# Attention on one Trainium2 core: ones beside the value tiles, every shift on GpSimd, normalisation on ScalarE, loads by 8 heads

## The chip, the cores and the metric

The kernel runs on one core of a Trainium2 chip. The metric is the device time of one execution in microseconds (us); lower is better. Each core has five engines with their own instruction queues: TensorE (PE; its weight loads are listed apart as PEld), VectorE (DVE), ScalarE (ACT), GpSimd (POOL) and SyncE (SP), which here only issues DMAs. The 16 DMA engines of the core move data between HBM and the on-chip memory SBUF. Matmul results go to PSUM.

## The reference

```python
B, H, Sq, Sk, D = 16, 32, 192, 1024, 128        # q: (B,H,Sq,D); k, v: (B,H,Sk,D); bf16

def reference(q, k, v):
    scale = q.shape[-1] ** -0.5
    scores = jnp.einsum("bhqd,bhkd->bhqk", q, k) * scale
    p = _softmax(scores, axis=-1)
    return jnp.einsum("bhqk,bhkd->bhqd", p, v)
```

There are 512 independent heads, and each is a whole softmax attention of 192 queries over 1024 keys.

## The kernel before

**Units.** Two heads make a pair, and a pair makes three units of 128 rows by 1024 keys: queries 0 to 127 of the first head (j = 0), queries 0 to 127 of the second (j = 1), and the last 64 queries of both heads stacked (j = 2). There are 256 pairs and 768 units. In the code `k3` is this j before the change.

**What is done to a unit.** `qk` (TensorE) makes the scores of the unit in PSUM (`s_ps`, two buffers), as two matmuls of 512 columns, for j = 2 as two column-tiled pairs. `rowmax` (VectorE, L300) copies them to SBUF (`ss`, four buffers), times minus the scale, and keeps the row's minimum in `nb`. Then a unit goes one of two ways, by `ROUTES = (R_W, R_W, R_EA)`. Units j = 0 and 1 (`R_W`): GpSimd subtracts the minimum (`shift`, L188, a tensor_tensor against a broadcast column) into `x_sb`; TensorE transposes in eight blocks of 128x128 (`tr`, L244) into `pt_ps`; ScalarE takes the exponential on the way out of PSUM into `pt_sb` (`evac`, L367). Unit j = 2 (`R_EA`): ScalarE takes the exponential before the transposes (`exp_first`, L356), with the row sums as a by-product in `rs`, and copies behind them (L369). `pv` (TensorE) multiplies the eight transposed blocks with the value tiles `vs` into `o_ps` (L267 for j = 0, 1; L273 and L275 for j = 2). For `R_W` units each such matmul is followed by one with a single column of ones against the same weights (L270), which gathers the row sums in slot 3 of `o_ps`. `onorm` (VectorE, L327 and L330) takes the reciprocals of a pair's sums and multiplies the pair's three outputs into `ob`.

**Order.** Each engine's program is written out by hand, one step a unit, with lags: in a step TensorE does `qk` of unit step+1, `tr` of unit step-4 and `pv` of unit step-7. VectorE does `rowmax` of the step's unit and `onorm` 8 steps behind the pair's last unit. Semaphores carry the dependences: `s_qk`, `s_max`, `s_xp` and `s_xa`, `s_tr`, `s_eva`, `s_pv`, `s_on`.

**Loads and stores.** All DMAs are issued by SP, in one order. A group is G = 16 heads, and NS = 2 groups have buffers, 32 heads in all. `loads(g)` issues the transposing load of K (L141, 4 MB), that of Q (L144, 0.79 MB) and the plain load of V (L149, 4 MB); for each partition and head, V's 8 rows of 128 values are 2,048 bytes in one run in HBM and in `vs` alike. Ahead of K it waits until the scores of the group that held the buffer are done, ahead of V until that group's `pv` is. `stores(g)` waits for the group's normalised output and issues three DMAs (L158, L163, L164), 0.79 MB in runs of 256 bytes. The order is `loads(g + NS)`, then `stores(g)`, for each g.

Of the kernel before, what the change touches and what calls it, by code (L numbers as in the profile page):

```python
# [6 lines left out]
F32 = mybir.dt.float32  # L7
ACT_FN = mybir.ActivationFunctionType
ALU = mybir.AluOpType

R_EA = 0
R_ED = 1
R_W = 2


def _attention_kernel(nc, q, k, v, out, G=16, NS=2, LAGS=(2, 4, 5, 7), ROUTES=(R_W, R_W, R_EA)):
# [4 lines left out]
    assert NH % G == 0 and G % 2 == 0  # L21
# [3 lines left out]
    NU = NGR * UPG  # L25
    KT_TILES = SK // 128
    scale = float(D) ** -0.5

    L_X, L_TR, L_EV, L_PV = LAGS
    assert 1 <= L_X < L_TR < L_EV < L_PV  # L30
# [4 lines left out]
    NRS = 4  # L35

# [5 lines left out]
    def route(u):  # L42
        return ROUTES[u % len(ROUTES)]

    x_cnt = []
    ev_cnt = []
    n_xa = n_xp = n_ea = n_ed = 0
    for u in range(NU):
        r = route(u)
        if r == R_W:  # L50
            n_xp += 1
            x_cnt.append(n_xp)
        else:
            n_xa += 1
            x_cnt.append(n_xa)
        if r == R_ED:
            n_ed += 1
            ev_cnt.append(n_ed)
        else:
            n_ea += 1  # L60
            ev_cnt.append(n_ea)

    with ExitStack() as es:
# [11 lines left out]
        vs = sb("vs", [128, NS, G, KT_TILES, 128], BF16)  # L75
        ob = sb("ob", [128, NSO, PPG, 4, 128], BF16)
# [3 lines left out]
        pt_sb = sb("pt_sb", [128, NPT, KT_TILES, 128], BF16)  # L80
# [5 lines left out]
        pt_ps = [ps("pt_ps%d" % i, [128, KT_TILES, 128], BF16) for i in range(2)]  # L86
        o_ps = [ps("o_ps%d" % i, [128, 4, 128], F32) for i in range(2)]
# [7 lines left out]
        s_xa = sem("s_xa")  # L95
        s_xp = sem("s_xp")
        s_tr = sem("s_tr")
        s_eva = sem("s_eva")
        s_evd = sem("s_evd")
# [6 lines left out]
        def unit_info(u):  # L106
            pr = u // 3
            k3 = u % 3
            g = pr // PPG
            pg = pr % PPG  # L110
            return pr, k3, g, pg

        O_SLOT = (0, 2, 1)

        def load_cnt(g):
            return 16 * (g // NS + 1)

        def store_cnt(g):
            return 48 * (g // NSO + 1)

        def wait_x(eng, u):
            if route(u) == R_W:
                eng.wait_ge(s_xp, x_cnt[u])
            else:
                eng.wait_ge(s_xa, x_cnt[u])

        def wait_evac(eng, u):
            if route(u) == R_ED:
                eng.wait_ge(s_evd, ev_cnt[u])
            else:  # L130
                eng.wait_ge(s_eva, ev_cnt[u])

        @block.sync
        def _(e):
            def loads(g):
                s = g % NS
                last_u = (g - NS + 1) * UPG - 1
                h0 = g * G
                if g >= NS:
                    e.wait_ge(s_qk, last_u + 1)  # L140
                e.dma_start_transpose(  # L141
                    kt[:, s], kf[h0:h0 + G].rearrange("g k d -> (g k) d")
                ).then_inc(sxk[s], 16)
                e.dma_start_transpose(  # L144
                    qt[:, s], qf[h0:h0 + G].rearrange("g k d -> (g k) d")
                ).then_inc(sxq[s], 16)
                if g >= NS:
                    e.wait_ge(s_pv, last_u + 1)
                e.dma_start(  # L149
                    vs[:, s], vf[h0:h0 + G].rearrange("g (p t) d -> p g t d", t=KT_TILES)  # L150
                ).then_inc(svl[s], 16)

            def stores(g):
                so = g % NSO
                e.wait_ge(s_on, (g + 1) * PPG)
                h0 = g * G
                og = of[h0:h0 + G]
# [10 lines left out]
            for g in range(NGR):  # L168
                if g + NS < NGR:
                    loads(g + NS)  # L170
                stores(g)
            for so in range(min(NSO, NGR)):
                n_uses = len(range(so, NGR, NSO))
                e.wait_ge(sst[so], 48 * n_uses)

        @block.gpsimd
        def _(gp):
# [4 lines left out]
            ).then_inc(s_setup, 1)  # L182

            def shift(u):
                gp.wait_ge(s_max, u + 1)
                if u >= NX:
                    gp.wait_ge(s_tr, u - NX + 1)
                gp.tensor_tensor(  # L188
                    x_sb[:, u % NX, :], ss[:, u % NSS, :],
                    nb[:, u % NSS: u % NSS + 1].to_broadcast([128, SK]), ALU.subtract,  # L190
                ).then_inc(s_xp, 1)

            for u in range(NU):
                if route(u) == R_W:
                    shift(u)

        @block.tensor
        def _(pe):
            def qk(u):
                pr, k3, g, pg = unit_info(u)  # L200
                s = g % NS
                if u % UPG == 0:
                    pe.wait_ge(sxk[s], load_cnt(g))
                    pe.wait_ge(sxq[s], load_cnt(g))
# [6 lines left out]
                for c in range(2):  # L211
                    cs = slice(512 * c, 512 * c + 512)
                    if k3 < 2:
                        x = a if k3 == 0 else b
                        ins = pe.matmul(  # L215
                            S[:, cs],
                            qt[:, s, x * SQ: x * SQ + 128],
                            kt[:, s, x * SK + 512 * c: x * SK + 512 * c + 512],
                            start=True, stop=True,
                        )  # L220
                    else:
                        pe.matmul(  # L222
                            S[0:64, cs],
                            qt[:, s, a * SQ + 128: a * SQ + 192],
                            kt[:, s, a * SK + 512 * c: a * SK + 512 * c + 512],
                            start=True, stop=True, tile_position=(0, 0),
                        )
                        ins = pe.matmul(  # L228
                            S[64:128, cs],
                            qt[:, s, b * SQ + 128: b * SQ + 192],  # L230
                            kt[:, s, b * SK + 512 * c: b * SK + 512 * c + 512],
                            start=True, stop=True, tile_position=(0, 64),
                        )
                ins.then_inc(s_qk, 1)

            def tr(u):
                wait_x(pe, u)
                if u >= 2:
                    wait_evac(pe, u - 2)
                X = x_sb[:, u % NX, :]  # L240
                PT = pt_ps[u % 2]
                ins = None
                for t in range(KT_TILES):
                    ins = pe.transpose(PT[:, t, :], X[:, t: SK: KT_TILES], ident[:])  # L244
                ins.then_inc(s_tr, 1)

            def pv(u):
                pr, k3, g, pg = unit_info(u)
                s = g % NS
                if u % UPG == 0:  # L250
                    pe.wait_ge(svl[s], load_cnt(g))
                wait_evac(pe, u)
                if k3 == 0 and pr >= 2:
                    pe.wait_ge(s_on, pr - 1)
                O = o_ps[pr % 2]
                PTS = pt_sb[:, u % NPT]
                sl = O_SLOT[k3]
                a = 2 * pg
                b = 2 * pg + 1
                ins = None  # L260
                with_rs = route(u) == R_W
                for t in range(KT_TILES):
                    first = t == 0
                    last = t == KT_TILES - 1
                    if k3 < 2:
                        x = a if k3 == 0 else b
                        ins = pe.matmul(O[:, sl, :], PTS[:, t, :], vs[:, s, x, t, :],  # L267
                                        start=first, stop=last, skip_group_check=True)
                        if with_rs:
                            ins = pe.matmul(O[:, 3, sl: sl + 1], PTS[:, t, :], ones[:, 0:1],  # L270
                                            start=False, stop=last, skip_group_check=True)
                    else:
                        pe.matmul(O[0:64, sl, :], PTS[:, t, 0:64], vs[:, s, a, t, :],  # L273
                                  start=first, stop=last, skip_group_check=True, tile_position=(0, 0))
                        ins = pe.matmul(O[64:128, sl, :], PTS[:, t, 64:128], vs[:, s, b, t, :],  # L275
                                        start=first, stop=last, skip_group_check=True, tile_position=(0, 64))
                        if with_rs:
                            pe.matmul(O[0:64, 3, sl: sl + 1], PTS[:, t, 0:64], ones[:, 0:1],
                                      start=False, stop=last, skip_group_check=True, tile_position=(0, 0))
                            ins = pe.matmul(O[64:128, 3, sl: sl + 1], PTS[:, t, 64:128], ones[:, 0:1],  # L280
                                            start=False, stop=last, skip_group_check=True, tile_position=(0, 64))
                ins.then_inc(s_pv, 1)

            pe.wait_ge(s_setup, 2)
# [10 lines left out]
        def _(dve):  # L295
# [9 lines left out]
            def evac(u):  # L305
                dve.wait_ge(s_tr, u + 1)
                if u >= NPT:
                    dve.wait_ge(s_pv, u - NPT + 1)
                dve.tensor_copy(pt_sb[:, u % NPT], pt_ps[u % 2][:]).then_inc(s_evd, 1)

            ri_total = [0]

            def onorm(pr):
                g = pr // PPG
                pg = pr % PPG
                so = g % NSO
                dve.wait_ge(s_pv, 3 * pr + 3)
                if pg == 0 and g >= NSO:
                    dve.wait_ge(sst[so], store_cnt(g - NSO))
# [96 lines left out]
```

## Time and profile before

| | us |
|---|---|
| median of 3 runs | 1264.91 |
| lowest, highest | 1264.91, 1265.55 |
| span of the profiled execution, first to last instruction | 1263.1 |
| PE busy; PEld busy | 1234.2; 1009.4 |
| DVE busy; ACT busy; POOL busy | 1102.0; 1048.6; 960.4 |
| first matmul starts | 21.0 |

The profiled execution is read by its span, 1263.1 us; the median of the runs stands 1.8 us above it, and what lies outside the span has no row. Busy times are sums over one execution. Matmuls are pipelined, so TensorE's busy time is not its time at peak. A DMA's issue (SPq rows) can last long because the queue takes no more until earlier transfers have drained. One pair takes 4.80 us in the steady state, and eight pairs (16 heads) take 38.4 us.

### The profile page before, as it was taken

Reading aid. Unit: us, or ns where it says so; the run is one execution under the profiler, and the core shown is the slowest. Engines: PE = TensorE matmul, PEld = TensorE weight load, DVE = VectorE, ACT = ScalarE, POOL = GpSimd, SP = SyncE. Lnnn points to the kernel's source line nnn. Section 1 sums busy time; section 2 is a strip of 40 time slices with the busy share of each in tenths; the row PEclk is TensorE's granted clock in tenths of the full one; section 3 lists DMA queues with packets and bytes.
Section 4 is the critical chain, followed back from the end, with each engine's and each line's share of the span. In section 5 each row is a group of like instructions: output and inputs, shape, how many; then the busy total and the mean of one; then the engine's idle time right before and its main releaser. Section 6 shows DMA issues by size and latency. Waiting matters only on the chain.

```text
span 1263.1 us, 48658 instructions
## 1 busy us (share of the span) xinstructions
PE 1234.2 (98%) x20480; PEld 1009.4 (80%) x20480; DVE 1102.0 (87%) x2304; ACT 1048.6 (83%) x1281; POOL 960.4 (76%) x518
## 2 busy tenths in 40 slices
PE   3999999999999999999999999999999999999997
PEld 1888888888888888888888888888888888888886
DVE  2889888898988989898898988889898898989885
ACT  1888888888888888888888888888888888888886
POOL 2778777777877778787777877777787777878774
PEclk9999999999999999999999999999999999999999
DMA  9999999999999999999999999999999999999941
GB/s 288 268 261 240 278 280 266 288 270 245 254 269 261 279 233 255 281 275 262 261 230 272 271 276 268 252 251 272 272 267 281 253 263 252 271 261 281 244 118 27
DMA packets 790743, 321.89 MB, mean 255 GB/s; under 512 B 724992, under 2 KB 724992, under 8 KB 790528
## 3 DMA queue, kind: packets, MB, share of 16 engines
q1 hardware_dynamic: 790528, 318.78, 108.8%
q8 instruction: 164, 2.69, 0.8%
q14 instruction: 51, 0.42, 0.1%
HBM read 134.22 MB, written 25.17 MB: 126 GB/s over the span
## 4 chain that ended last, share of the span: by engine, by line
PE 97%; SPq 1%; DMA 1%; ACT 0%; issue 0%; DVE 0%; ACTq 0%
PE pt_ps L244 33%; PE o_ps L267 24%; PE s_ps L215 18%; PE o_ps L273 11%; PE s_ps L222 9%; SPq L141 1%; DMA vs<-in_v_dram 1%; PE o_ps L270 1%; PE o_ps L275 1%; SPq L144 0%; PE s_ps L228 0%; ACT x_sb L356 0%; ACT pt_sb L367 0%; DVE ob L330 0%; DVE rinv L327 0%
## 5 line engine op out<-in xcount | busy, mean ns | idle before, releaser
L188 POOL TENSOR_TENSOR x_sb<-ss,nb 128x1024 bf16<-128x1024 f32 x512 | 959.7, 1895 | 288.9 <-PE pt_ps L244 266.8
L300 DVE TENSOR_SCALAR_CACHE_REDUCE ss<-s_ps 128x1024 f32<-128x1024 f32 x768 | 938.5, 1222 | 140.5 <-PE s_ps L215 110.8
L244 PEld LDWEIGHTS pt_ps<-ident,x_sb 128*128 128x128 bf16 x6144 | 487.1, 148 | 203.3 <-issue 105.4
L367 ACT ACTIVATE pt_sb<-pt_ps 128x1024 bf16<-128x1024 bf16 x512 | 521.0, 1018 | 41.9 <-PE pt_ps L244 41.8
L244 PE MATMUL pt_ps<-ident,x_sb 128*128 128x128 bf16 x6144 | 520.7, 228 | 0.2 <-ACT pt_sb L367 0.2
L267 PE MATMUL o_ps<-vs,pt_sb 128*128 128x128 bf16 x4096 | 403.0, 217 | 0.3 <-DMA vs<-in_v_dram 0.3
L369 ACT ACTIVATE pt_sb<-pt_ps 128x1024 bf16<-128x1024 bf16 x256 | 262.1, 1024 | 140.1 <-PE pt_ps L244 140.0
L270 PE MATMUL o_ps<-ones,pt_sb 128*128 128x1 bf16 x4096 | 376.0, 165 | 0.0
L267 PEld LDWEIGHTS o_ps<-vs,pt_sb 128*128 128x128 bf16 x4096 | 352.3, 97 | 0.5 <-DMA vs<-in_v_dram 0.4
L270 PEld LDWEIGHTS o_ps<-ones,pt_sb 128*128 128x128 bf16 x4096 | 340.7, 96 | 0.0
L215 PE MATMUL s_ps<-kt,qt 128*128 128x512 bf16 x1024 | 305.3, 379 | 21.3 <-DMA qt<-in_q_dram 21.0
L356 ACT ACTIVATE x_sb<-ss,nb 128x1024 bf16<-128x1024 f32 x256 | 292.3, 1142 | 23.6 <-DVE ss L300 23.6
L273 PE MATMUL o_ps<-vs,pt_sb 128*64 128x128 bf16 x2048 | 162.3, 222 | 0.0
L275 PE MATMUL o_ps<-vs,pt_sb 128*64 128x128 bf16 x2048 | 162.3, 222 | 0.0
L222 PE MATMUL s_ps<-kt,qt 128*64 128x512 bf16 x512 | 153.2, 381 | 0.6 <-DVE ss L300 0.5
L228 PE MATMUL s_ps<-kt,qt 128*64 128x512 bf16 x512 | 153.2, 381 | 0.0
L330 DVE TENSOR_TENSOR ob<-o_ps,rinv 128x384 bf16<-128x384 f32 x256 | 142.7, 557 | 8.7
L273 PEld LDWEIGHTS o_ps<-vs,pt_sb 128*64 128x64 bf16 x2048 | 121.0, 109 | 17.1
L275 PEld LDWEIGHTS o_ps<-vs,pt_sb 128*64 128x64 bf16 x2048 | 121.0, 109 | 0.0
L215 PEld LDWEIGHTS s_ps<-kt,qt 128*128 128x128 bf16 x1024 | 63.3, 96 | 23.6 <-issue 21.5
L300 DVE DVE_READ_ACCUMULATOR ss<-s_ps 128x1 f32 x768 | 64.0, 83 | 0.0
L356 ACT ACTIVATION_READ_ACCUMULATOR x_sb<-ss,nb 128x1 f32 x256 | 48.9, 191 | 0.0
(11 smaller groups left out, 165.7 us busy)
## 6 DMA issues: line engine op xcount, KB each, us to landing
vs<-in_v_dram SPq DMA_DIRECT2D x32, 4096.0 KB, 15.2
out_dram<-ob SPq DMA_DIRECT2D x32, 512.0 KB, 15.9
out_dram<-ob SPq DMA_DIRECT2D x64, 128.0 KB, 4.9
kt<-in_k_dram SPq DMA_TRANSPOSE x32, 21.4
qt<-in_q_dram SPq DMA_TRANSPOSE x32, 6.6
```

The lines of the kernel that those rows point to most:

```text
L188: gp.tensor_tensor(x_sb[:, u % NX, :], ss[:, u % NSS, :], nb[:, u % NSS: u % NSS + 1].to_broadcast([128, SK]), ALU.subtract,).then_inc(s_x ...
L215: ins = pe.matmul(S[:, cs], qt[:, s, x * SQ: x * SQ + 128], kt[:, s, x * SK + 512 * c: x * SK + 512 * c + 512], start=True, stop=True,)
L222: pe.matmul(S[0:64, cs], qt[:, s, a * SQ + 128: a * SQ + 192], kt[:, s, a * SK + 512 * c: a * SK + 512 * c + 512], start=True, stop=True, ...
L244: ins = pe.transpose(PT[:, t, :], X[:, t: SK: KT_TILES], ident[:])
L267: ins = pe.matmul(O[:, sl, :], PTS[:, t, :], vs[:, s, x, t, :], start=first, stop=last, skip_group_check=True)
L270: ins = pe.matmul(O[:, 3, sl: sl + 1], PTS[:, t, :], ones[:, 0:1], start=False, stop=last, skip_group_check=True)
L273: pe.matmul(O[0:64, sl, :], PTS[:, t, 0:64], vs[:, s, a, t, :], start=first, stop=last, skip_group_check=True, tile_position=(0, 0))
L275: ins = pe.matmul(O[64:128, sl, :], PTS[:, t, 64:128], vs[:, s, b, t, :], start=first, stop=last, skip_group_check=True, tile_position=(0, ...
L300: dve.tensor_scalar(ss[:, u % NSS, :], s_ps[u % 2][:], -scale, None, ALU.mult, ALU.min, accum_out=nb[:, u % NSS: u % NSS + 1],).then_inc(s ...
L356: act.activation(x_sb[:, u % NX, :], ss[:, u % NSS, :], ACT_FN.Exp, bias=nb[:, u % NSS: u % NSS + 1], scale=-1.0, accum_out=rs[:, pr % NRS ...
L367: act.activation(pt_sb[:, u % NPT], pt_ps[u % 2][:], ACT_FN.Exp, scale=-1.0).then_inc(s_eva, 1)
L369: act.activation(pt_sb[:, u % NPT], pt_ps[u % 2][:], ACT_FN.Copy).then_inc(s_eva, 1)
```

## The change

- **Row sums.** `vs` gets rows of `VW = 130` values instead of 128, and GpSimd writes ones into the two spare columns once at the start. A `pv` matmul takes 129 columns, so that column 128 of its output is the row sum. The matmuls of L270 are gone.
- **One way for all units.** `TYPES = (W, W, W)`: GpSimd shifts all 768 units, ScalarE takes all exponentials behind the transposes. The shift is a tensor_scalar, times -1 plus `nb`, instead of a tensor_tensor; the exponential no longer has a scale of -1.
- **Normalisation.** VectorE does one reciprocal a pair; ScalarE does three multiplications a pair (Copy with a scale per row), each counted in `s_on`.
- **Loads.** G = 8 and NS = 4, again 32 heads of buffers. K and Q still go as one transposing DMA each a group; V goes as one DMA a head, whose destination has 128 values and a gap of 2 (runs of 256 bytes). Stores still go by 16 heads (`GO`).

The lags are as before. The core of the diff:

```diff
-def _attention_kernel(nc, q, k, v, out, G=16, NS=2, LAGS=(2, 4, 5, 7), ROUTES=(R_W, R_W, R_EA)):
+TYPES = (W, W, W)
+def _attention_kernel(nc, q, k, v, out, G=8, NS=4, GO=16, L_X=2, L_TR=4, L_EV=5, L_PV=7):
...
+    VW = D + 2
...
-        vs = sb("vs", [128, NS, G, KT_TILES, 128], BF16)
+        vs = sb("vs", [128, NS, G, T, VW], BF16)
...
-        o_ps = [ps("o_ps%d" % i, [128, 4, 128], F32) for i in range(2)]
+        o_ps = [ps("o_ps%d" % i, [128, 3, VW], F32) for i in range(2)]
...
                 if g >= NS:
                     e.wait_ge(s_pv, last_u + 1)
-                e.dma_start(
-                    vs[:, s], vf[h0:h0 + G].rearrange("g (p t) d -> p g t d", t=KT_TILES)
-                ).then_inc(svl[s], 16)
+                for i in range(G):
+                    e.dma_start(
+                        vs[:, s, i, :, 0:D], vf[h0 + i].rearrange("(p t) d -> p t d", t=T)
+                    ).then_inc(svl[s], 16)
...
             for g in range(NGR):
                 if g + NS < NGR:
                     loads(g + NS)
-                stores(g)
+                if (g + 1) % (GO // G) == 0:
+                    stores((g + 1) // (GO // G) - 1)
...
+            gp.memset(vs[:, :, :, :, D:VW], 1.0).then_inc(s_setup, 1)
...
-                gp.tensor_tensor(
+                gp.tensor_scalar(
                     x_sb[:, u % NX, :], ss[:, u % NSS, :],
-                    nb[:, u % NSS: u % NSS + 1].to_broadcast([128, SK]), ALU.subtract,
-                ).then_inc(s_xp, 1)
+                    -1.0, nb[:, u % NSS: u % NSS + 1], ALU.mult, ALU.add,
+                ).then_inc(s_x[W], 1)
...
-                        ins = pe.matmul(O[:, sl, :], PTS[:, t, :], vs[:, s, x, t, :],
-                                        start=first, stop=last, skip_group_check=True)
-                        if with_rs:
-                            ins = pe.matmul(O[:, 3, sl: sl + 1], PTS[:, t, :], ones[:, 0:1],
-                                            start=False, stop=last, skip_group_check=True)
...
+                for t in range(T):
+                    for r, m, x in rows:
+                        tp = {} if j < 2 else {"tile_position": (0, r)}
+                        ins = pe.matmul(
+                            O[r:r + m, sl, 0:D + 1], P[:, t // 2, t % 2, r:r + m], vs[:, s, x, t, 0:D + 1],
+                            start=t == 0, stop=t == T - 1, skip_group_check=True, **tp)
...
+            def recip(pr):
                 dve.wait_ge(s_pv, 3 * pr + 3)
+                if pr >= 2:
+                    dve.wait_ge(s_on, ON * (pr - 1))
...
+                        src = o_ps[pr % 2][:, c, D]
+                    dve.reciprocal(rinv[:, pr % 2, c], src).then_inc(s_ri, 1)
...
-                dve.tensor_tensor(
-                    ob[:, so, pg, 0:3, :],
-                    o_ps[pr % 2][:, 0:3, :],
-                    rinv[:, pr % 2, 0:3].unsqueeze(2).to_broadcast([128, 3, 128]),
-                    ALU.mult,
-                ).then_inc(s_on, 1)
...
+            def norm(pr):
+                so = pr // PPO % NSO
+                act.wait_ge(s_ri, RECIPS * (pr + 1))
+                if pr % PPO == 0 and pr // PPO >= NSO:
+                    act.wait_ge(sst[so], 48 * (pr // PPO // NSO))
+                for sl in range(3):
+                    act.activation(
+                        ob[:, so, pr % PPO, sl, :], o_ps[pr % 2][:, sl, 0:D], ACT_FN.Copy,
+                        scale=rinv[:, pr % 2, sl:sl + 1],
+                    ).then_inc(s_on, 1)
+            for step in range(NU + L_PV + 3):
                 u = step - L_EV
-                if 0 <= u < NU and route(u) != R_ED:
+                if 0 <= u < NU:
                     evac(u)
...
+                u = step - L_PV - 1
+                if 0 <= u < NU and u % 3 == 2:
+                    norm(u // 3)
```

## The prediction

> **What bounds the kernel now.** First the page: engine shares, the slices, the chain that ended last, and the costliest groups.
>
> ```profile
> PE 1234.2 (98%) x20480; PEld 1009.4 (80%) x20480; DVE 1102.0 (87%) x2304; ACT 1048.6 (83%) x1281; POOL 960.4 (76%) x518
> ...
> DMA  9999999999999999999999999999999999999941
> ...
> q1 hardware_dynamic: 790528, 318.78, 108.8%
> q8 instruction: 164, 2.69, 0.8%
> ...
> PE 97%; SPq 1%; DMA 1%; ACT 0%; issue 0%; DVE 0%; ACTq 0%
> ...
> L188 POOL TENSOR_TENSOR x_sb<-ss,nb 128x1024 bf16<-128x1024 f32 x512 | 959.7, 1895 | 288.9 <-PE pt_ps L244 266.8
> ```
>
> The chain is TensorE for 97%. But the DMA engines are full in every slice up to the last two, and the chain alone can't tell how near they are to bounding. So next the timeline of SP's own queue, for one 16-head group and the start of the next (start, us, instruction):
>
> ```profile
> 902.61 18.25 SPq L141 DMA_TRANSPOSE kt<-in_k_dram  x1
> 920.91 3.98 SPq L144 DMA_TRANSPOSE qt<-in_q_dram  x1
> 924.93 0.59 SPq L149 DMA_DIRECT2D vs<-in_v_dram  x1
> 925.57 4.52 SPq L158 DMA_DIRECT2D out_dram<-ob  x1
> 930.13 9.94 SPq L163 DMA_DIRECT2D out_dram<-ob  x1
> 940.12 0.64 SPq L164 DMA_DIRECT2D out_dram<-ob  x1
> 940.80 17.73 SPq L141 DMA_TRANSPOSE kt<-in_k_dram  x1
> ```
>
> SP goes from one DMA to the next with no gap. The long rows are not waits for compute (the scores that this K load needs had ended at 901.5): the last stores of the run, with nothing in front of them, issue in 0.4 to 1.3 us each, so L163's 9.9 us is V still draining. K of the fourth group issues at 101.85 and of the 26th at 940.80: 22 cycles of 38.1 us. TensorE needs 38.4 us for 16 heads. Two resources are within 1% of each other; a change that relieves one and loads the other goes by the other.
>
> Third, the windows view, for the rates (window, length, ..., DMA share, GB/s): a K load alone at the start, V alone, the last stores alone.
>
> ```profile
> 6.00:16.00 10.00, 0.00 (x0) 0.00 (x0) 0.00 (x0) 0.00 (x0) 0.00 (x0) 1.00 1.28 290
> ...
> 626.00:632.00 6.00, 6.00 (x104) 4.97 (x104) 5.16 (x12) 4.74 (x7) 3.90 (x3) 1.00 1.05 396
> ...
> 1258.50:1260.50 2.00, 0.00 (x0) 0.00 (x0) 0.00 (x0) 0.00 (x0) 0.00 (x0) 0.79 0.97 220
> ```
>
> V, in packets of 2,048 bytes, moves at 396 GB/s. K's transposes, in packets of 256, at 290: 256 B / (290/16 GB/s) = 14.1 ns a packet and engine. The stores, plain copies with rows of 256 bytes, at 220: 18.6 ns.
>
> **TensorE.** The chain in order of time gives the pitch of a value matmul:
>
> ```profile
> 603.36 0.05 PE o_ps L273
> ...
> 604.77 0.08 PE o_ps L267
> ```
>
> With a ones matmul behind it one takes 0.080 us, without (j = 2) 0.055. The change takes away 16 such followers a pair: 16 x 0.025 = 0.39 us; the 129th column adds 1/128 of 0.055 to 24 pitches, 0.01. A pair goes from 4.80 to 4.42 us, 16 heads from 38.4 to 35.4, the run loses 256 x 0.38 = 97 us. Rows that start 260 bytes apart have no row here; at worst the gain is lost (the old 0.080 pitch). K and Q for 8 heads in place of 16 let the first matmul start at about 11.4 us instead of 21.0: 9.6 more. TensorE alone would end at 1263.1 - 97 - 10 = 1156 us.
>
> **V's loads: the term that decides.** A run of V in `vs` shrinks from 2,048 to 256 bytes by the gap of two ones. The packet size of the old load equals the shorter of its two runs (2,048 in HBM, far longer in `vs`), so I take packets of 256 now, eight times as many: 16,384 for 16 heads. 16 heads of V are 4.19 MB. At 396 GB/s that is 10.6 us; at the transposes' 14.1 ns, 14.5 us; at the stores' 18.6 ns, 19.0 us. Neither row is a plain load of 256-byte rows; one shares its direction, the other its form, so I take the middle, 16.8.
>
> The Trainium skill ("DMA: Bandwidth & Descriptors", Why small descriptors are slow) counts 8 + 3 cycles for a 256-byte packet, 12.9 ns at its 850 MHz; an estimate from that page would be 13.2 us for V, a cycle of 39.7 and, by the sum below, 1290 us. Both rows here are slower than it says, and its Specifications ask for 512 bytes for full rate, which speaks against this change.
>
> **Instruction fetches.** The 164 packets of q8 are 16 KB each, and TensorE has 40,960 of the 48,658 instructions. In the windows view 608 to 610 us falls to 109 GB/s just behind one of these packets: (1 - 109/290) x 2 = 1.25 us lost. Without 8,192 matmuls and weight loads there are 33 fewer, at most 41 us, or 1.3 us a 16-head cycle; VectorE's and ScalarE's lists change by a few hundred instructions. I take 1.0 (0 to 1.3).
>
> **The new DMA cycle.** 38.1 - 10.6 + 16.8 - 1.0 = 43.3 us for 16 heads; from 38.1 - 10.6 + 14.5 - 1.3 = 40.7 to 38.1 - 10.6 + 19.0 = 46.5. TensorE's 35.4 is below all of them: the loads become the bound.
>
> Of the moved loads, what SP issues: 16 V DMAs a cycle at 0.59 us, 9.4 us, beside 16.8 us of transfer, so issue stays ahead. The new order has V's wait for `s_pv` behind each half-size K and Q; `pv` lags the scores by 14 us (group 22: 901.5 and 915.5) while K and Q of 8 heads take 11. If TensorE set the pace SP would stand there some 3 us a group with the next K queued behind it. When loads set it, TensorE has been idle for the wanted group and the wait is over before SP comes to it: nothing. The same holds for the stores' wait.
>
> **The other engines, by 16 heads (8 pairs).**
> - GpSimd: 24 shifts instead of 16. The tensor_scalar has no row. From below: the set-up memset of 128 elements takes 0.20 us against 0.10 for one, 0.8 ns an element, so 0.93 us. The affine_select, one input and more arithmetic, takes 0.29: 1.5 ns, so 1.64. From above: the tensor_tensor with two inputs, pitch 1.875 (two in 3.75). Likeliest near 1.2, between the first two: 29 us; 1.64 gives 39.4; 1.875 gives 45.0. It binds over 43.3/24 = 1.80 us. The spare-column memset, 512 elements, lies within the first load.
> - VectorE: loses the multiplication and one reciprocal, keeps 3 row maxima at a pitch of 1.35 and about 0.2: 34 us.
> - ScalarE: loses exp_first (1.14 + 0.19), gains three normalisations of 128 columns. Its rows are 1.02 for 1024 columns and 0.19 for one, 0.81 ns a column: 0.29 each, 0.41 if the per-row scale adds what separates 1.14 from 1.02. 8 x 3 x 1.43 = 34 us at most. `norm` waits for a reciprocal, which comes behind a row maximum; the next exponentials stand behind it, about 0.4 us late. `pv` asks for them three units after the transposes, 4.4 us against 1 us of work, so this costs nothing; without that cover, 256 x 0.4 = 102 us.
>
> **The end.** DMA data starts at 2.0 us. K and Q of the last 8 heads have landed when all but the last V (8.4) and three stores (3 x 3.6) are through: 2 + 32P - 19. Then 12 units of 1.47 us (17.7), 9.5 from the last scores to the last `pv` (1247.1 to 1256.6 now), 6.5 to the end. Span = 32P + 17, with P = 43.3: 1403 us, and 1.8 more for the median: 1405. The bounds of P give 1321 and 1507.
>
> **Rivals.**
> *Faster: the small rows cost nothing.* If the DMA engine still reads V in 2,048-byte pieces and the split on the write side is hidden, P = 38.1 - 1.0 = 37.1 and the median is 1206 us; TensorE's 1156 is hidden below it. It decides from P = 38.9, V at 12.4 us or 338 GB/s; between 338 and 396 lies the whole faster side. For it: 2,048-byte packets reach 396 GB/s, so the SBUF side can. Against: nothing in 256-byte packets here goes over 290.
> *The shift binds.* At the tensor_tensor's pitch 768 x 1.875 = 1440, with 13 us before the first and 12 behind the last: 1465 us. For it: same engine, same bytes. Against: one streamed input less, and both one-input rows are cheaper. The skill's "GPSIMD Engine Reference" (Engine selection) calls one-input operations "roughly line-rate"; an estimate from its 1.2 GHz would be 0.85 us; the set-up rows lie above that.
> *Rows dearer than any shown.* V's rows now start at addresses that are multiples of 4, not 256. At 24 ns a packet V takes 24.6, P = 51.1, 1654 us.
> *The wait on `s_pv` idles the queue* adds up to 3 us a group only if the first rival holds: 64 x 3 = 192 us on 1206 at most, back to slower; in part, about the old time.
>
> **How the numbers follow.** The forecast (256-byte packets at 14 to 19 ns) has 0.57 and its own range is 1321 to 1507. The shift as the bound has 0.12 and falls into it. Dearer rows, over 1507, have 0.13. The rival on the other side has 0.15, and no change 0.03; what a measurement of this kernel can tell from no change is about 0.2%, 2.5 us. From 1200 to 1510 us the dearer rows and a little of the faster side are left out. Faster 0.15, same 0.03, slower 0.82.
>
> **What would show it.** Right: packets under 512 bytes rise from 724,992 to about 1,250,000; "DMA vs<-in_v_dram" or "DMA kt/qt" appear in the chain, PE falls below 90% busy with idle time before L215's successor in each 8-head group, and SP's cycle for two groups is about 43 us. The value matmul's pitch should be 0.056, the shift about 1.2 us, ScalarE's normalisation about 0.3 to 0.4. Wrong: V in 2,048-byte packets, V windows over 338 GB/s, a chain that stays on PE or moves to POOL, or a shift over 1.8 us.

## The result, and the profile after

The changed kernel takes 1481.22 us, the median of 4 runs (1477.97 to 1483.49), against 1264.91 before: 1.171 times the old time, 95% interval 1.169 to 1.172. The forecast was 1405, with a range of 1200 to 1510. The profiled execution has a span of 1478.4 us.

First the packets of the kernel before:

```profile
DMA packets 790743, 321.89 MB, mean 255 GB/s; under 512 B 724992, under 2 KB 724992, under 8 KB 790528
```

Then the page of the changed kernel: engine shares, slices, packets, the chain that ended last, the shift's and the normalisation's groups.

```profile
PE 1215.2 (82%) x16384; PEld 960.8 (65%) x16384; DVE 973.0 (66%) x1792; ACT 963.7 (65%) x1537; POOL 860.6 (58%) x775
...
DMA  9999999999999999999999999999999999999992
...
DMA packets 1259198, 321.46 MB, mean 217 GB/s; under 512 B 1259008, under 2 KB 1259008, under 8 KB 1259008
...
q1 hardware_dynamic: 1259008, 318.82, 114.9%
q8 instruction: 132, 2.16, 0.7%
...
PE 56%; SPq 31%; DMA 7%; ACT 4%; issue 2%; ACTq 0%; DVE 0%
...
L166 POOL TENSOR_SCALAR x_sb<-ss,nb 128x1024 bf16<-128x1024 f32 x768 | 859.4, 1119 | 605.0 <-PE pt_ps L216 591.7
...
L319 ACT ACTIVATE ob<-o_ps,rinv 128x128 bf16<-128x128 f32 x768 | 224.9, 368 | 271.5 <-DMA out_dram<-ob 264.4
```

No engine is busier than 82%; the DMA row alone is full in every slice but the last. The bytes are the same as before (318.8 MB on q1), but all of them now go in packets of less than 512 bytes, 1,259,008 against 724,992. TensorE's share of the chain has fallen from 97% to 56%, and SP's queue and DMAs together have 38% of it.

The last group shows something that the prediction did not have: ScalarE stands 264 us before normalisations, waiting for stores to land.

Next the timeline of SP's queue in the changed kernel, one cycle of 16 heads and the start of the next (start, us, instruction):

```profile
719.21 7.85 SPq L118 DMA_TRANSPOSE kt<-in_k_dram  x1
727.10 1.47 SPq L121 DMA_TRANSPOSE qt<-in_q_dram  x1
728.61 9.30 SPq L127 DMA_DIRECT2D vs<-in_v_dram  x8
737.95 9.58 SPq L118 DMA_TRANSPOSE kt<-in_k_dram  x1
747.57 1.34 SPq L121 DMA_TRANSPOSE qt<-in_q_dram  x1
748.96 10.59 SPq L127 DMA_DIRECT2D vs<-in_v_dram  x8
759.59 1.10 SPq L135 DMA_DIRECT2D out_dram<-ob  x1
760.73 2.01 SPq L140 DMA_DIRECT2D out_dram<-ob  x1
762.78 0.75 SPq L141 DMA_DIRECT2D out_dram<-ob  x1
763.58 8.45 SPq L118 DMA_TRANSPOSE kt<-in_k_dram  x1
```

SP again goes from one DMA to the next with no gap, and it does not stand for compute: over the whole run each K load was issued 41 us or more after the scores that free its buffer had ended. It stands because the queue is full. V's sixteen DMAs take 20 us of its time. This cycle lasts 44.4 us; the mean of 23 cycles, from one K issue to the next, is 45.35, against 38.08 before.

The windows view of the changed kernel gives the rates, first while V lands, then while K's transposes do:

```profile
753.00:758.00 5.00, 5.00 (x72) 4.00 (x71) 4.14 (x9) 3.98 (x7) 3.84 (x4) 1.00 1.36 220
743.00:748.00 5.00, 5.00 (x81) 4.07 (x81) 4.35 (x8) 3.96 (x7) 3.64 (x5) 1.00 1.27 290
```

V moved at 396 GB/s before and moves at 220 now. That is 256 B / (220/16 GB/s) = 18.6 ns a packet and engine, the very rate of the stores. K's 290 is unchanged.

The mean granted clock fell from 0.999 to 0.913. That is not what sets the cycle: the loads do not wait for TensorE, and in both windows above TensorE is busy throughout at a clock of 1.00. Lower values stand where it idles and starts again: 0.88 from 760 to 766 us, where it is busy for 0.60 us, and 0.50 from 766 to 770, where it is busy for 2.05.

### The profile page after: what moved, and what is told of

It reads as the page before. It is cut to its first block, busy times and chain, and to the rows that moved or that the text cites. A ratio compares the mean times of both kernels' runs of the same rounds, so it can differ in the third digit from the quotient of the medians.

```text
span 1478.4 us, 41297 instructions
## 1 busy us (share of the span) xinstructions
PE 1215.2 (82%) x16384; PEld 960.8 (65%) x16384; DVE 973.0 (66%) x1792; ACT 963.7 (65%) x1537; POOL 860.6 (58%) x775
## 2 busy tenths in 40 slices
DMA packets 1259198, 321.46 MB, mean 217 GB/s; under 512 B 1259008, under 2 KB 1259008, under 8 KB 1259008
## 3 DMA queue, kind: packets, MB, share of 16 engines
q1 hardware_dynamic: 1259008, 318.82, 114.9%
## 4 chain that ended last, share of the span: by engine, by line
PE 56%; SPq 31%; DMA 7%; ACT 4%; issue 2%; ACTq 0%; DVE 0%
PE pt_ps L216 21%; SPq L127 20%; PE o_ps L236 19%; PE s_ps L192 10%; DMA out_dram<-ob 6%; PE s_ps L200 6%; SPq L140 5%; SPq L135 3%; SPq L118 2%; ACT pt_sb L308 2%; ACT ob L319 2%; SPq L121 1%; DMA kt<-in_k_dram 1%; ACTq L306 0%; ACTq L317 0%
## 5 line engine op out<-in xcount | busy, mean ns | idle before, releaser
L166 POOL TENSOR_SCALAR x_sb<-ss,nb 128x1024 bf16<-128x1024 f32 x768 | 859.4, 1119 | 605.0 <-PE pt_ps L216 591.7
L216 PEld LDWEIGHTS pt_ps<-ident,x_sb 128*128 128x128 bf16 x6144 | 501.0, 149 | 459.8 <-issue 346.9
L216 PE MATMUL pt_ps<-ident,x_sb 128*128 128x128 bf16 x6144 | 543.9, 235 | 231.3 <-ACT pt_sb L308 231.3
L236 PE MATMUL o_ps<-vs,pt_sb 128*128 128x129 bf16 (+1 forms) x8192 | 514.6, 230 | 0.0
L236 PEld LDWEIGHTS o_ps<-vs,pt_sb 128*128 128x128 bf16 (+1 forms) x8192 | 407.7, 109 | 20.9 <-ACT pt_sb L308 5.4
L319 ACT ACTIVATE ob<-o_ps,rinv 128x128 bf16<-128x128 f32 x768 | 224.9, 368 | 271.5 <-DMA out_dram<-ob 264.4
L192 PE MATMUL s_ps<-kt,qt 128*128 128x512 bf16 x1024 | 312.7, 388 | 24.5 <-DMA qt<-in_q_dram 12.5
L278 DVE RECIPROCAL rinv<-o_ps 128x3 f32<-128x3 f32 x256 | 45.0, 176 | 263.7 <-PE o_ps L236 263.7
L200 PE MATMUL s_ps<-kt,qt 128*64 128x512 bf16 x1024 | 167.8, 410 | 0.6 <-DVE ss L257 0.5
L192 PEld LDWEIGHTS s_ps<-kt,qt 128*128 128x128 bf16 x1024 | 81.5, 99 | 27.6 <-issue 25.5
L200 PEld LDWEIGHTS s_ps<-kt,qt 128*64 128x64 bf16 x1024 | 47.4, 118 | 2.5 <-DVE ss L257 2.4
## 6 DMA issues: line engine op xcount, KB each, us to landing
kt<-in_k_dram SPq DMA_TRANSPOSE x64, 12.5
```

The lines of the kernel that those rows point to most:

```text
L166: gp.tensor_scalar(x_sb[:, u % NX, :], ss[:, u % NSS, :], -1.0, nb[:, u % NSS: u % NSS + 1], ALU.mult, ALU.add,).then_inc(s_x[W], 1)
L192: ins = pe.matmul(S[:, c:c + 512], qt[:, s, x * SQ: x * SQ + 128], kt[:, s, x * SK + c: x * SK + c + 512], start=True, stop=True,)
L200: ins = pe.matmul(S[r:r + 64, c:c + 512], qt[:, s, x * SQ + 128: x * SQ + 192], kt[:, s, x * SK + c: x * SK + c + 512], start=True, stop=T ...
L216: ins = pe.transpose(PT[:, 128 * t: 128 * t + 128], X[:, t::T], ident[:])
L236: ins = pe.matmul(O[r:r + m, sl, 0:D + 1], P[:, t // 2, t % 2, r:r + m], vs[:, s, x, t, 0:D + 1], start=t == 0, stop=t == T - 1, skip_grou ...
L278: dve.reciprocal(rinv[:, pr % 2, c], src).then_inc(s_ri, 1)
```

## The experiments

The expectations use three theories. **T1**: V's 256-byte packets set the time. **T2**: the output buffers do: ScalarE cannot normalise until stores that sit in SP's queue behind two groups of loads have landed, and TensorE stands behind it. **T3**: loading by 8 heads does, since the queue changes twice as often between transposes and copies.

**Dense V in the changed kernel.**

```diff
-    VW = D + 2
+    VW = D
...
-                            O[r:r + m, sl, 0:D + 1], P[...], vs[:, s, x, t, 0:D + 1],
+                            O[r:r + m, sl, 0:D], P[...], vs[:, s, x, t, 0:D],
```

> The changed kernel with value rows of 128 again, so that V goes in runs of 2,048 bytes (still one DMA a head); the row sums are left out (the reciprocal reads output column 0 in their place). Theory 1 (V's 256-byte packets set the time through the DMA queue): the cycle for 16 heads falls from 45.5 us by 19.1 - 10.6 = 8.5 to about 37.0, the run to 32 x 37.0 + 17 = 1200 us (1190 to 1250), packets under 512 B back to about 725,000. Theory 2 (the wait of the normalisation for the stores to land, 264 us in ScalarE's queue, sets it): the stores still stand behind a load group in the queue, so most of the wait stays, 1400 us or more. Theory 3 (loads by 8 heads cost the queue its pace): 1400 us or more.

Measured: 1280.27 us, 1.012 times before (1.010 to 1.014). From the page of this kernel:

```profile
DMA packets 800446, 321.46 MB, mean 251 GB/s; under 512 B 734720, under 2 KB 734720, under 8 KB 800256
...
PE 65%; SPq 19%; DMA 8%; ACT 5%; issue 2%; DVE 0%; ACTq 0%
```

The gap, with the ones column that stands in it, is worth 201 of the 216 us. T2 and T3, which keep everything else, had asked for over 1400, and fall as the main cause. But T1's own number, 1200, is missed by 80 us: something beside the gap costs too.

**The gap alone, in the kernel before.**

```diff
-        vs = sb("vs", [128, NS, G, KT_TILES, 128], BF16)
+        vs = sb("vs", [128, NS, G, KT_TILES, 130], BF16)
...
+                for i in range(G):
+                    e.dma_start(vs[:, s, i, :, 0:128], vf[h0 + i]...).then_inc(svl[s], 16)
```

> The kernel before with one thing of the change: value rows 130 apart and one V DMA a head (runs of 256 bytes); the matmuls read 128 columns, all else as before. Theory 1: 38.1 + 8.5 = 46.6 us a cycle, 32 x 46.6 + 17 = 1508 us (1480 to 1540), slower than the whole change because it keeps the instruction fetches. Theories 2 and 3: within 1% of 1265.

Measured: 1521.69 us, 1.202 times before (1.200 to 1.204), a loss of 256 us. From its page, the chain by engine:

```profile
SPq 47%; PE 41%; DMA 10%; issue 2%; ACT 0%; DVE 0%; ACTq 0%
```

The old engine code, all its ones matmuls included, is slower than the whole change when its V has the gap, and TensorE falls from 97% to 41% of the chain. The cycle is 46.59 us, 8.51 longer than before. The stores' rate gives 19.0 - 10.6 = 8.4 for the same 4.19 MB: the price is that row, not the middle. This run also splits V into one DMA a head; run j below does that without the gap, and its cycle is 38.03, so the split alone does not cost this.

**Output buffers by 8 heads.** The buffers hold 32 heads as before, but in four pieces, so that the stores that a normalisation waits for stand in SP's queue behind no loads but those that its own heads need anyway.

```diff
-def _attention_kernel(nc, q, k, v, out, G=8, NS=4, GO=16, ...):
+def _attention_kernel(nc, q, k, v, out, G=8, NS=4, GO=8, ...):
...
-    NSO = 2
+    NSO = 4
```

> The changed kernel with four output buffers of 8 heads instead of two of 16, stores by 8 heads. Theory 1: the DMA queue is full either way; the same 1481 us within 1.5% (1460 to 1490), while the wait of the normalisation for the stores moves or shrinks. Theory 2: the 264 us go, 1220 to 1300 us.

Measured: 1506.67 us, 1.190 times before (1.185 to 1.194); not a gain but 25 us more. The waits of this kernel (engine, line, waited for: us, times, longest):

```profile
PEld s_ps L192 <- issue: 259.6, 66, 12.5
PE s_ps L192 <- issue: 237.1, 63, 6.6
```

and its chain:

```profile
DMA 49%; PE 41%; issue 6%; SPq 4%; ACT 0%; ACTq 0%; DVE 0%
DMA kt<-in_k_dram 49%; PE pt_ps L216 14%; PE o_ps L236 13%; PE s_ps L192 10%; PE s_ps L200 3%; SPq L118 2%; SPq L127 2%; SPq L121 0%; ACT pt_sb L308 0%; ACT ob L319 0%; ACTq L58 0%; DVE rinv L278 0%
```

ScalarE's wait for stores is gone from the list, and 260 us have come up at TensorE's next scores (L192), which now wait for K (49% of the chain). The idle time moved and did not shrink. The output buffer is where the full queue shows first, not what costs the time, so T2 falls altogether. T1's own 1460 to 1490 is missed as well: the cycle is 46.64, 1.29 longer than in the changed kernel. What stores in pieces of 8 heads cost the queue was not tried alone.

**Loads by 8 heads, in the kernel before.** The stores go by G too, so this also halves the output buffer.

```diff
-def _attention_kernel(nc, q, k, v, out, G=16, NS=2, ...):
+def _attention_kernel(nc, q, k, v, out, G=8, NS=4, ...):
```

> The kernel before with one thing of the change: loads by 8 heads over four buffers (V one DMA a group in runs of 2,048 bytes, stores by 8 heads). Theory 1: TensorE's 4.80 us a pair stays the bound, the first matmul starts about 9 us earlier: 1253 to 1260 us. Theory 3: the queue loses its pace, over 1290 us.

Measured: 1320.31 us, 1.042 times before (1.039 to 1.046): 55 us, where T1 saw a gain. Its waits contain one that the list of the kernel before does not have:

```profile
DVE rinv L327 <- DMA out_dram<-ob: 94.7, 47, 26.4
```

VectorE waits 95 us for the halved output buffer, so this run does not separate the loads from the stores. The next two do.

**Loads by 16 heads in the changed kernel,** all else kept, first with the gap:

```diff
-def _attention_kernel(nc, q, k, v, out, G=8, NS=4, GO=16, ...):
+def _attention_kernel(nc, q, k, v, out, G=16, NS=2, GO=16, ...):
```

> The changed kernel with loads by 16 heads over two buffers again (V still one DMA a head with 256-byte runs). Theory 1 with a second term (each change of the queue from plain copies to transposes loses DMA time, so loads by 8 heads cost about 2 us a 16-head cycle): 45.5 - 2.0 = 43.5 us a cycle, 1395 to 1430 us. Theory 1 alone (only V's packets matter): 1465 to 1485 us.

Measured: 1484.85 us, 1.173 times before (1.172 to 1.175), cycle 45.73: no difference from the change. With 256-byte packets the size of the loads costs nothing, and the second term that run a had asked for is not there.

**The same with dense V** (both edits, a and e):

> The dense kernel (changed kernel, value rows of 128, row sums left out) with loads by 16 heads over two buffers. It completes the square of {gap, no gap} x {8, 16 heads}. If loads by 8 heads cost the queue 2 us a cycle where V is dense: 37.1 us a cycle and 1205 to 1230 us. If not: 1270 to 1290 us as with 8 heads, and something else in the change keeps the dense queue at 39.2.

Measured: 1239.27 us, 0.979 times before (0.977 to 0.981), cycle 38.03; 41 us below the dense kernel with loads by 8 (cycle 38.97, 0.94 more), and between the two forecasts. So loads by 8 do cost, but only where V is dense. That is 41 of the 80 us by which run a had missed; most of the rest is that the dense cycle is 38.03 even with loads by 16, where T1 had 37.0 (32 x 1.03 = 33 us). It also repeats the main finding at 16 heads: e less j is the gap with its ones, 246 us.

**The length of a run.** Ones between every two value rows, so that two rows lie together as 512 bytes; a matmul takes its ones from the left or from the right, and VectorE adds the two half sums.

```diff
+        BLK = 2 * D + 2
+        vsf = sb("vs", [128, NS * G * (T // 2) * BLK + 2], BF16)
...
+                        c0 = ((s * G + x) * (T // 2) + t // 2) * BLK + (1 if t % 2 == 0 else 2 + D)
+                        z = t % 2
...
+                            O[r:r + m, sl, z:z + D + 1], P[...], vsf[:, c0:c0 + D + 1],
```

> The changed kernel with ones between every two value rows, so that V goes in runs of 512 bytes; an even block takes its row sum from the ones ahead of its values, an odd one from those behind, and VectorE adds the two sums (two more small operations a pair). If a packet costs a fixed part plus its bytes (83 ns at 2,048 bytes and 18.8 at 256 make 9.6 ns + 0.036 ns a byte), 512 bytes cost 28 ns and V 14.3 us for 16 heads: 43% of the way from the dense kernel's 1280 to 1481, 1365 us (1345 to 1390). If packets from 512 bytes run at full rate, 1280 us within 1.5%.

Measured: 1371.3 us, 1.084 times before (1.082 to 1.086). Two windows of this kernel's V loads:

```profile
716.00:722.00 6.00, 6.00 (x86) 4.78 (x83) 5.51 (x15) 5.16 (x11) 4.34 (x5) 1.00 1.00 268
737.00:741.00 4.00, 4.00 (x64) 3.33 (x63) 3.58 (x9) 3.38 (x7) 2.90 (x4) 1.00 1.10 279
```

In the first window 1,016 of Q's 256-byte packets still come in; the second is V alone. At 279 GB/s a 512-byte packet takes 512 / (279/16) = 29.4 ns. Against 18.6 for 256 bytes and 82.7 for 2,048 (396 GB/s) that is nearly one straight line, some 10 ns and 0.036 ns a byte (10 + 18.4 = 28.4 at 512). The times follow: 1481, 1371 and 1280 us for runs of 256, 512 and 2,048 bytes. None of the shorter two is free.

**Only the ones matmuls left out, in the kernel before.**

```diff
-                        if with_rs:
-                            ins = pe.matmul(O[:, 3, sl: sl + 1], PTS[:, t, :], ones[:, 0:1], ...)
```

> The kernel before without its 4,096 ones matmuls (row sums of two units in three left out, output column 0 in their place); all else as before. TensorE falls to 4.42 us a pair, 35.4 us a 16-head cycle, and 33 fewer instruction fetches save the queue 1.0 us: 38.1 - 1.0 = 37.1 us, 1205 to 1225 us. If the fetches save nothing: 38.1 us, 1237 to 1250 us. If TensorE alone counted: 1165 us.

Measured: 1234.88 us, 0.976 times before (0.973 to 0.980), cycle 37.75. The chain of this kernel:

```profile
PE 73%; DMA 18%; SPq 5%; issue 3%; ACT 0%; DVE 0%; ACTq 0%
```

TensorE is busy for 86 us less (1234.2 to 1148.1; the forecast had 97), and the time falls by 30: DMAs enter the chain at once. The packets of q8 fall from 164 to 132, and the cycle by 0.33 us, not by the 1.0 that the forecast gave to them; so the time lies just under what was expected if the fetches save nothing. The cycles account for less than half of the 30 us. The last K load is issued 12.6 us earlier (1157.78 against 1170.34); the other 17 are gained behind it, where TensorE works off the heads that are loaded.

**V's loads on a second queue** (ScalarE's), in the changed kernel:

```diff
+                    if u % UPG == UPG - 1 and u // UPG + NS < NGR:
+                        act.wait_ge(s_pv, u + 1)
+                        vloads(act, u // UPG + NS)
```

> The changed kernel with V's loads, from the fifth group on, issued from ScalarE's queue instead of SP's, at the point where the pv that frees the buffer is done. Theory 1 in its narrow form (time of the 16 DMA engines a packet): the engines are full either way, 1440 to 1490 us. Rival (the single in-order queue with its stalls between transposes and copies): the two queues fill each other's stalls, below 1400 us.

Measured: 1777.85 us, 1.405 times before (1.403 to 1.408). Neither expectation holds. The chain of this kernel, and ScalarE's timeline:

```profile
PE 57%; ACTq 30%; ACT 9%; issue 2%; SPq 1%; DMA 1%; DVE 0%
...
704.14 10.34 ACTq L113 DMA_DIRECT2D vs<-in_v_dram  x7
714.58 1.94 ACT L312 ACTIVATE pt_sb<-pt_ps 128x1024 bf16<-128x1024 bf16 x2 [10.10 <-issue]
```

ScalarE itself stands 10 us in its issues, and 30% of the chain lies in such issues. The run tells what a full queue does to an engine that has other work. Whether two queues would move 256-byte packets faster it does not tell.

**The first 16 heads in four pieces, in the kernel before,** for the forecast's 9.6 us at the start:

```diff
+            for c in range(NPC):            # NPC = 4, four heads a piece
+                e.dma_start_transpose(kt[:, 0, ...], kf[h:h + HP]...).then_inc(sk0[c], 16)
+                e.dma_start_transpose(qt[:, 0, ...], qf[h:h + HP]...).then_inc(sq0[c], 16)
+                e.dma_start(vs[:, 0, h:h + HP], vf[h:h + HP]...).then_inc(sv0[c], 16)
```

> The kernel before with its first 16 heads loaded in four pieces of 4 heads (K, Q, V each), so that TensorE can start at about 6 us instead of 21. If TensorE's 4.80 us a pair alone bounds the kernel before: 1265 - 15 = 1250 us. If the DMA queue's 38.1 us a cycle is as near a bound as the prediction said (32 x 38.1 + 17 to 23, and three more changes from copies to transposes): 1243 to 1260 us with TensorE now waiting for loads in the steady state.

Measured: 1273.7 us, 1.007 times before (1.004 to 1.009); both expectations had a gain. SP's timeline at the start of this kernel, the last piece and the second group, and a window of the engines:

```profile
27.86 7.08 SPq L173 DMA_TRANSPOSE kt<-in_k_dram  x1
34.98 1.29 SPq L176 DMA_TRANSPOSE qt<-in_q_dram  x1
36.32 1.54 SPq L179 DMA_DIRECT2D vs<-in_v_dram  x1
37.90 19.92 SPq L146 DMA_TRANSPOSE kt<-in_k_dram  x1
```

```profile
50.00:60.00 10.00, 0.00 (x0) 0.00 (x0) 0.00 (x0) 0.00 (x0) 0.52 (x1) 0.64 1.28 282
```

TensorE begins at 8.4 us and then stands idle from 50 to 60 us, because the second group's K, issued at 19.52 before, is issued at 37.90. Here an early first matmul was worth nothing, because the next load came later.

**A version that beats both.** What relieves TensorE without touching V: the second unit of a pair also takes the exponential ahead of the transposes, and ScalarE's copy behind them goes by 32-bit words.

```diff
-def _attention_kernel(nc, q, k, v, out, G=16, NS=2, LAGS=(2, 4, 5, 7), ROUTES=(R_W, R_W, R_EA)):
+def _attention_kernel(nc, q, k, v, out, G=16, NS=2, LAGS=(2, 4, 5, 7), ROUTES=(R_W, R_EA, R_EA)):
...
-                    act.activation(pt_sb[:, u % NPT], pt_ps[u % 2][:], ACT_FN.Copy).then_inc(s_eva, 1)
+                    act.copy(pt_sb[:, u % NPT]....bitcast(I32), pt_ps[u % 2]....bitcast(I32)).then_inc(s_eva, 1)
```

> A version meant to beat both: the kernel before with two units in three exponentiated ahead of the transposes (row sums for nothing) and one shifted, and ScalarE's copy behind the transposes read as 512 32-bit integers. Half of the ones matmuls go: TensorE 4.6 us a pair, ScalarE about 4.4, VectorE 4.5; the DMA queue at 37.6 us a cycle is then the bound, 1225 to 1255 us. If the 32-bit copy is no faster than the 16-bit one, ScalarE takes 5.1 us a pair: 1330 us or more.

Measured: 1254.47 us, 0.992 times before (0.990 to 0.995). The copy's group in this kernel:

```profile
L370 ACT COPY pt_sb<-pt_ps 128x512 int32<-128x512 int32 x512 | 298.0, 582 | 121.5 <-PE pt_ps L245 121.5
```

The copy takes 582 ns where the same bytes as 16-bit values took 1024 (L369 before); the instruction also changed, from ACTIVATE to COPY, and the two were not tried apart. It is a small gain, since its cycle, 38.21 us, is the loads': each K load was issued 10 us or more after the scores that free its buffer, all but the first. The gain comes behind the last K load, from whose issue to the end of the span it takes 76.4 us (1250.7 - 1174.27) instead of 92.8 (1263.1 - 1170.34).

## Why the prediction was right, and which terms were off

**The bound.** Right: V's small rows turn the loads into the bound. Taking the gap out of the change gives back 201 us (246 with loads by 16), and putting it alone into the old kernel costs 256.

**V's price.** The mechanism was right, the size too small. The two rows were 14.1 and 18.6 ns a packet, and the forecast took their middle, +6.2 us a cycle. The upper row is the price: 220 GB/s in the window, +8.51 in run c. Like V, the stores are plain copies in rows of 256 bytes; their direction, the reason given for going below them, made no difference. The term is not quite additive: e less j gives 7.70, the changed kernel less a 6.38. Why is open.

**Instruction fetches.** With 32 fewer the cycle is 0.33 us shorter in run k and 0.05 in run j, which has as few. The saving is at most a third of the 1.0 taken, but within its 0 to 1.3. The hole in the rate that the forecast priced at 1.25 us a fetch is thus for the greater part not lost time in this kernel.

**The sum.** The cycle was forecast at 43.3 and measured at 45.35: 32 x 2.05 = 66 us. By the terms, V at the stores' rate would add 2.2 us to the cycle and the smaller saving on fetches 0.7, together 0.8 more than the 2.05 measured: the same open point as above. The constant behind 32 cycles was forecast at 17 and measured at 1478.4 - 32 x 45.35 = 27: 10 us. 1403 + 66 + 10 = 1479. So both mis-sized terms erred towards too short a time, and the measured 1481 lies near the upper end of the forecast's own 1321 to 1507. Part of the 10 lies in the last group, whose scores take 25.8 us (1437.4 to 1463.2) instead of 17.7.

**Where the wait shows.** Here a sign was wrong. TensorE was to wait for K and Q; instead ScalarE's first normalisation of an output group waits for stores, as its timeline in the changed kernel shows:

```profile
753.15 0.88 ACT L319 ACTIVATE ob<-o_ps,rinv 128x128 bf16<-128x128 f32 x3
766.01 0.88 ACT L319 ACTIVATE ob<-o_ps,rinv 128x128 bf16<-128x128 f32 x3 [8.30 <-DMA out_dram<-ob]
```

The group of stores at 759.59 in SP's queue was ready at 709.4, when its last normalisation ended, and had loads for two coming groups ahead of it. "The same holds for the stores' wait" was argued from SP waiting for compute; it overlooked compute waiting for SP. As run b shows, it cost nothing that the queue did not cost anyway.

**What else held.** The packets (1,259,008 against "about 1,250,000"), PE below 90% (82), the shift (1.119 us against 1.2, so GpSimd is 58% busy and does not bind), the normalisation (0.368 us within 0.29 to 0.41). Where nothing stalls, the normalisations of successive pairs begin 4.45 us apart (four steps from 735.34 to 753.15), against a predicted 4.42; the first matmul starts at 12.5 us, against 11.4; eight value matmuls take 0.47 to 0.48 us in the chain, 0.059 each against 0.056. That rows 260 bytes apart could slow TensorE down does not show.

**Loads by 8 heads** cost nothing, as forecast, but only with the gap (45.35 against 45.73 in run e): in dense V they cost 0.94 us a cycle and 41 us (a against j). It is not the wait on `s_pv` that the prediction priced for this case: in run a each V load was issued 31 us or more after the `pv` that frees its buffer. The extra time shows in V's own transfers: from the first packet of a load to its last, 16 heads of V take 14.3 us in run a, in two loads, and 13.3 in run j, in one. Had the first rival held, its 1206 us would have been missed for this reason and because the dense cycle is 38.03 and not 37.1 even with loads by 16: run a is that rival made true, and took 1280.

**The other rivals.** Small rows are not free: V's windows never came near the 338 GB/s from which that side began. Nor were they dearer than the stores', so starting at multiples of 4 bytes has no price that shows.

## What to carry to other kernels

When two resources stand within 1% of each other, ask of each edit what it does to the second one before counting what it saves on the first: 86 us less of TensorE's busy time were worth 30 alone, and the whole change cost 216 net with a gap in the loads' destination. Count the runs on both sides of a DMA; the shorter one makes the packet, and the nearest plain copy in the profile with such rows gives its price. When an engine waits for a buffer, take that wait away before believing that it is the cause: a full queue shows at whichever buffer runs out first.

## What the runs showed of the hardware that was not expected

- A packet's time grew almost linearly from 256 to 2,048 bytes (18.6, 29.4, 82.7 ns). The Trainium skill ("DMA: Bandwidth & Descriptors", Specifications) asks for 512 bytes or more for full rate; run f has 512 bytes throughout V and moves at 279 GB/s, against 396 at 2,048, so here the measurement decides against the page.
- The hole behind an instruction fetch seemed to be 1.25 us, and leaving out 32 of them shortened the queue's cycle by 0.33 us at most, 0.33 each.
- An engine that issues DMAs into a full queue stands: seven issues took ScalarE 10.34 us.
- Loads by 8 heads instead of 16 cost 0.94 us a cycle with 2,048-byte packets of V and nothing with 256-byte ones. Why V's transfers take longer in two loads than in one was not found.
- ScalarE's COPY of a unit from PSUM by 32-bit words took 57% of the time of its ACTIVATE of the same bytes as 16-bit values (582 and 1024 ns).
